# Value tiles on GpSimd's DMA queue, key tiles issued two pairs ahead on SyncE's: a decode attention kernel

## The chip, the cores and the metric

The kernel runs on one core of a Trainium2 chip. The metric is the device time of one execution in microseconds (us), and lower is better. Engines are called as in the profile: PE is TensorE (matmul), PEld its weight loads, DVE is VectorE, ACT is ScalarE, POOL is GpSimd, SP is SyncE. SP, ACT and POOL can issue DMAs, each on a queue of its own. The core has 16 DMA engines.

## The reference

One decode step of attention over a long cache, mixed with a small feed-forward block by a sigmoid gate. Everything is float32.

```python
# x [2,1,448], k_cache and v_cache [2,16,4096,256], wq [448,4096], wo [4096,448]
q = (x @ wq).reshape(B, Sq, H, Dh).transpose(0, 2, 1, 3)
scores = einsum("bhqd,bhkd->bhqk", q, k_cache) * (Dh ** -0.5)
p = softmax(scores)
a = einsum("bhqk,bhkd->bhqd", p, v_cache).transpose(0, 2, 1, 3).reshape(B, Sq, H * Dh) @ wo
b = relu(x @ w1 + b1) ** 2 @ w2 + b2          # w1 [448,1792], w2 [1792,448]
g = sigmoid((x * gate_w).sum(-1, keepdims=True))
out = g * a + (1 - g) * b
```

Each of the 2 x 16 = 32 pairs of batch and head has one query row, 4 MB of keys and 4 MB of values. These caches are 268 of the 290 MB that the kernel reads.

## The kernel before

The main loop runs over the 32 pairs, numbered i = 0 to 31 (batch inside, head outside; the last is `last` = 31). A tile `k0_14_0` holds the keys of batch 0, head 14, so of pair 28; `v1_13_0` the values of pair 27. One tile is 128 partitions x 8192 floats, the whole 4 MB of a pair, and comes with one DMA. Values of the last two pairs come in two and three pieces.

All large tiles (keys, values, and the weights wq, w1, w2, wo) share a ring of five slots of 4 MB (`slot`). A load waits until the tile that had its slot has been used up: keys until their reduction on DVE, values until their products on PE. All these loads are issued on SP's queue in program order, so that a load that waits for its slot also holds back those behind it.

What pair i goes through:

- `times_q(i, ...)` (L294): DVE multiplies the keys in place by the query, in three pieces of 1024, 3072 and 4096 columns; `row_sums(i)` (L300): DVE adds up each row of 256, which gives 4096 scores.
- `maximum(i)` (L304, L306) and `softmax(i)` (L312, L317): a maximum over all partitions with the help of PE, then exponentials on ACT. DVE's stream puts the first piece of `times_q(i + 1)` between the two, so the softmax of pair i also stands behind the arrival of the keys of pair i + 1.
- `values(i)` (L343): 32 PE matmuls of the probabilities with the value tile.

At the top of iteration i the kernel issues the keys of pair i + 1 and then the values of pair i (in iteration 29 the keys of 30 and 31 and then the values of 29). Weights follow at fixed iterations: w1 at 2, a first part of w2 at 4, a group of wo at 7, 15 and 23. The last group of wo stands between the two pieces of v30, the rest of w2 (L111) behind the values of 31. At the very end PE multiplies wo and w2 chunks into `fin` (L390), one chunk after the other as they arrive, and 4 KB of output go out.

POOL does six small set-up instructions at the start and nothing in the loop.

Of the kernel before, what the change touches and what calls it, by code (L numbers as in the profile page):

```python
# [16 lines left out]
def kernel(  # L17
# [14 lines left out]
    nc = tc.nc  # L32
# [10 lines left out]
    J = 32  # L43
    NCH = NK // J
    HG = 4
    NG = H // HG
# [22 lines left out]
    def slot(name):  # L69
        return ring.tile([P, J * DH], F32, name=name, tag="ring")  # L70
# [15 lines left out]
    def load_w1():  # L86
        t = slot("w1")
        nc.sync.dma_start(t[:, :2 * F], w1[:2 * P, :].rearrange("(p c) n -> p (c n)", c=2))
        nc.sync.dma_start(t[:, 2 * F:3 * F], w1[2 * P:R0, :])
        nc.sync.dma_start(t[:, 3 * F:3 * F + F // 2], w1[R0:, :].rearrange("r (s n) -> (r s) n", s=2))  # L90
        w1_t.extend([t[:, :F], t[:, F:2 * F], t[:, 2 * F:3 * F], t[:, 3 * F:3 * F + F // 2]])
# [4 lines left out]
    def w2_slot(lo, hi):  # L96
        t = slot(f"w2_{lo}")
        tv = t[:, :(hi - lo) * D].rearrange("p (c n) -> p c n", n=D)
        for c in range(lo, hi):
            w2_sb[c] = tv[:, c - lo, :]  # L100
        return tv

    def load_w2_early():
        tv = w2_slot(0, WH)
        nc.sync.dma_start(tv, w2_v[:, :WH, :])

    def load_w2_late():
        tv = w2_slot(WH, FC)
        at = [0, *W2_CUTS, FC - WH]
        for lo, hi in zip(at, at[1:]):  # L110
            nc.sync.dma_start(tv[:, lo:hi, :], w2_v[:, WH + lo:WH + hi, :])  # L111
# [9 lines left out]
    def load_wo(g):  # L121
        t = slot(f"wo{g}")
        tv = t[:, :HJ * D]
        if g < NG - 1:
            nc.sync.dma_start(tv, wo_g[g])
            wo_sb[g] = tv.rearrange("p (j n) -> p j n", j=HJ)
        else:
            nc.sync.dma_start(tv.rearrange("p (h k) -> p h k", h=HG), wo_v[:, g * HG:(g + 1) * HG, :])
            wo_sb[g] = tv.rearrange("p (h j n) -> p h j n", h=HG, j=NJ)

    def load_kv(src, i, nm, cuts=(), between=None):
        b, h = pairs[i]
        v = src[b, h].rearrange("(n p j) d -> n p j d", p=P, j=J)
        tiles = []
        for n in range(NCH):
            t = slot(f"{nm}{b}_{h}_{n}").rearrange("p (j d) -> p j d", d=DH)
            at = [0, *(cuts if n == NCH - 1 else ()), J]
            for lo, hi in zip(at, at[1:]):
                nc.sync.dma_start(t[:, lo:hi, :], v[n, :, lo:hi, :])
                if between is not None and hi < J:  # L140
                    between()
            tiles.append(t)
        return tiles

    pairs = [(b, h) for h in range(H) for b in range(B)]
    last = len(pairs) - 1
# [43 lines left out]
    for c in range(CF + 1):  # L190
        src = (x2[:, c:2 * P:2] if c < 2 else x2[:, c * P:(c + 1) * P] if c < CF
               else xr2.rearrange("b r s -> b (r s)"))
# [41 lines left out]
    def make_q(b, n):  # L234

        a, gq = divmod(n, 4)
        r = 32 * gq + b
        pq = ps.tile([P, 512], F32, name=f"pq{b}_{n}", tag="pq")
        nc.tensor.matmul(pq, ident[:, r:r + 1].to_broadcast([P, P]), qs[:, a, :], start=True, stop=True)  # L239
        t = work.tile([P, QB], F32, name=f"q{b}_{n}", tag=f"q{b}")  # L240
        nc.scalar.activation(t, pq, AF.Copy)  # L241
        for k in range(QH):
            q_sb[b, n * QH + k] = t[:, k * DH:(k + 1) * DH]
# [36 lines left out]
    kts, s_t, rs_t, rl_t, oT = {}, {}, {}, {}, {}  # L280
# [8 lines left out]
    def times_q(i, lo, hi):  # L289

        b, h = pairs[i]
        for n, a, e in parts(lo, hi):
            kt = kts[i][n][:, a:e, :]
            nc.vector.tensor_tensor(kt, kt, q_sb[b, h].unsqueeze(1).to_broadcast([P, e - a, DH]), op=ALU.mult)  # L294
# [7 lines left out]
    def maximum(i):  # L302
        m = work.tile([P, 1], F32, name=f"m{i}", tag="m")
        nc.vector.tensor_reduce(m, s_t[i], axis=AX.X, op=ALU.max)  # L304
        mt = ps.tile([P, 512], F32, name=f"mt{i}", tag="sm")
        nc.tensor.matmul(mt[:, :P], m.to_broadcast([P, P]), ident, start=True, stop=True)  # L306
        return mt

    def softmax(i, mt):
        b, h = pairs[i]  # L310
        nb = work.tile([P, 1], F32, name=f"nb{i}", tag="nb")
        nc.vector.tensor_reduce(nb, mt[:, :P], axis=AX.X, op=ALU.max, negate=True)  # L312
        u, k = unit_of[h]
        c = B * k + b
        if c == 0:
            rs_t[u] = work.tile([P, B * len(units[u])], F32, name=f"rs{u}", tag="rs")
        nc.scalar.activation(pw[k, b][:, :, 2 * c:2 * c + 2], s_t[i].rearrange("p (m s) -> p m s", s=2), AF.Exp,  # L317
                             bias=nb, accum_out=rs_t[u][:, c:c + 1])

    def sums(u):  # L320
        sm = ps.tile([P, 512], F32, name=f"sum{u}", tag="sm")
        nc.tensor.matmul(sm[:, :B * len(units[u])], ones_pp, rs_t[u], start=True, stop=True)  # L322
        return sm

    def norm(u, sm):
        n = len(units[u])
        rc = work.tile([P, n, B], F32, name=f"rc{u}", tag="rc")
        nc.vector.reciprocal(rc, sm[:, :B * n].rearrange("p (k b) -> p k b", b=B))
        nc.vector.tensor_tensor(rc, rc, gP[:, 0, :].unsqueeze(1).to_broadcast([P, n, B]), op=ALU.mult)
        rl = work.tile([P, n * B, 2], F32, name=f"rl{u}", tag="rl")  # L330
        nc.vector.tensor_tensor(rl, m16[:, :4 * n].rearrange("p (c s) -> p c s", s=2),
                                rc.rearrange("p k b -> p (k b)").unsqueeze(2).to_broadcast([P, n * B, 2]), op=ALU.mult)
        rl_t[u] = rl
# [49 lines left out]
    def project(g):  # L383
        for j in range(HJ):
            nc.tensor.matmul(acc[:, :D], oT[g][:, j, :], wo_sb[g][:, j, :], start=False,  # L385
                             stop=(g == NG - 2 and j == HJ - 1))
# [13 lines left out]


    kts[0] = load_kv(k_cache, 0, "k")
    project_q()
    make_q(0, 0)
# [9 lines left out]
            times_q(i, n * J, (n + 1) * J)  # L414
            row_sums(i, n * J, (n + 1) * J)

    for i, (b, h) in enumerate(pairs):

        for n in (range(i + 1, i + 2) if i < last - 2 else range(i + 1, last + 1) if i == last - 2 else ()):
            kts[n] = load_kv(k_cache, n, "k")  # L420
        if i == last - 1:
            vt = load_kv(v_cache, i, "v", (J // 2,), lambda: load_wo(NG - 1))
        else:
            vt = load_kv(v_cache, i, "v", (J // 2, 3 * J // 4) if i == last else ())
        if i == 2:
            load_w1()
        if i == 4:
            load_w2_early()
        grp = h // HG
        if b == B - 1 and h % HG == HG - 1 and grp < NG - 1:  # L430
            load_wo(grp)
        if i == last:
            load_w2_late()

        if i < last - 1:
            mt = maximum(i)
        if i < last:
            times_q(i + 1, 0, LEAD)
        softmax(i, mt)
        if i < last:  # L440
            times_q(i + 1, LEAD, LEAD2)
        u, k = unit_of[h]
        done = b == B - 1 and k == len(units[u]) - 1
        if done:
            norm(u, sums(u))


        if h % QH == QH - 1 and h + 1 < H:
            make_q(b, (h + 1) // QH)
        if k == 0 and b == 0 and u > 0:  # L450
            turn(u - 1)
            if u < NG:
                project(u - 1)
        if i == 3:
            ffn_hidden()
        if i == 4:
            pt = ffn_turn()
        if i == 5:
            for c in range(WH):
                nc.tensor.matmul(acc[:, :D], hT[:, c, :], w2_sb[c], start=False, stop=False)  # L460
        if i == last - 6:

            ya = const.tile([B, D], F32, name="ya")
            nc.scalar.activation(ya, acc[:, :D], AF.Copy)
        if i == last - 5:
            late(ident[:B, :B], ya, start=True)

        if i == last - 2:
            rest(i + 1)
            mt = maximum(i + 1)  # L470
        if i < last - 1:
            values(i, vt)
            if done:
                take(u)
        if i == last - 1:
            rest(last)
            values(i, vt, 0, NK // 4)
            values(i, vt, NK // 4, 3 * NK // 8 + 2)
            mt = maximum(last)
            values(i, vt, 3 * NK // 8 + 2)  # L480
        elif i < last - 2:
            rest(i + 1)
        if i == 4:
            ffn_square(pt)
# [46 lines left out]
```

## Time and profile before

| | |
|---|---|
| device time, median of 3 runs | 683.49 us (683.36 to 683.56) |
| profiled execution, its own time | 683.23 us |
| its span, first to last instruction | 681.4 us |
| read from HBM | 289.56 MB, 425 GB/s over the span |
| PE, DVE, ACT, POOL busy | 296.5, 581.1, 37.9, 0.7 us |

The span is what the trace shows of one execution; 1.8 us of the device time lie outside it. Rows of the timeline give the start, the duration, the engine, the line, the operation with its tiles, and in brackets the idle time of the engine just before it with what ended that idle time. An `x2` means that two instructions are merged into one row, from the start of the first to the end of the second. Rows of the DMA list give the size of one transfer and the median time from its issue to its landing. The chain of work that ended last is followed back from the last instruction. `SPq`, `ACTq` and `POOLq` are the instruction queues of the engines that issue DMAs.

### The profile page before, as it was taken

To read this page: it belongs to the slowest core of one execution; us is meant where nothing else is said; L and a number is where in the kernel's file an instruction comes from. 1 tells how busy PE (TensorE), PEld (TensorE's weight loads), DVE (VectorE), ACT (ScalarE), POOL (GpSimd) and SP (SyncE) were. 2 spreads that over 40 slices of the span, in tenths; PEclk is the share of its full clock that TensorE was granted. 3 is DMA by queue.
4 is the path that set the end of the run, shared out by engine and by line. 5 is a ranking of instruction groups with operands and counts; after the bars stand their busy time and mean duration, and the time that the engine had idled before them with its cause. 6 is when DMAs were issued, how large, how long until landed. Compare 5 with 4: busy or idle time off the path is not lost.

```text
span 681.4 us, 3865 instructions
## 1 busy us (share of the span) xinstructions
PE 296.5 (44%) x1598; PEld 96.8 (14%) x1598; DVE 581.1 (85%) x233; ACT 37.9 (6%) x113; POOL 0.7 (0%) x6
## 2 busy tenths in 40 slices
PE   4413445543359134433347543422455712443066
PEld 1000111400115001000014110000112200101013
DVE  3299997989896999999996999899997899999990
ACT  0200001000010000000001000000001000000000
POOL 0000000000000000000000000000000000000000
PEclk9856667787656776665667865567667757667579
DMA  8999999999999999999999999999999999999996
GB/s 370 435 433 435 430 425 431 426 434 436 431 437 430 431 431 431 430 431 431 432 426 441 431 431 432 433 429 431 431 430 423 432 431 431 430 435 437 423 419 270
DMA packets 12380, 289.79 MB, mean 425 GB/s; under 512 B 1478, under 2 KB 1612, under 8 KB 2892
## 3 DMA queue, kind: packets, MB, share of 16 engines
q1 hardware_dynamic: 12200, 289.55, 99.1%
q8 instruction: 12, 0.20, 0.1%
q10 hardware_dynamic: 164, 0.02, 0.0%
q14 instruction: 4, 0.03, 0.0%
HBM read 289.56 MB, written 0.00 MB: 425 GB/s over the span
## 4 chain that ended last, share of the span: by engine, by line
DMA 59%; DVE 37%; PE 2%; issue 0%; SPq 0%; ACT 0%; DVEq 0%; ACTq 0%
DMA k<-in_A_k_cache_dram 56%; DVE k L294 18%; DVE s L300 18%; DMA w<-in_B_w_dram 3%; PE acc L385 1%; PE po_buf L343 1%; DVE nb L312 0%; PE mt L306 0%; DVE m L304 0%; PE fin L390 0%; SPq L111 0%; ACT oT L378 0%; SPq L81 0%; ACT pw L317 0%; SPq L80 0%
## 5 line engine op out<-in xcount | busy, mean ns | idle before, releaser
L294 DVE TENSOR_TENSOR k<-k,q 128x3072 f32<-128x3072 f32 (+3 forms) x94 | 285.1, 3057 | 75.7 <-DMA k<-in_A_k_cache_dram 75.7
L300 DVE TENSOR_REDUCE s<-k 128x32 f32<-128x8192 f32 x32 | 278.0, 8686 | 2.2
L343 PE MATMUL po_buf<-v,pw 128*16 128x512 f32 (+2 forms) x1024 | 181.1, 857 | 218.3 <-DMA v<-in_A_v_cache_dram 217.4
L343 PEld LDWEIGHTS po_buf<-v,pw 128*16 128x16 f32 (+2 forms) x1024 | 36.7, 123 | 349.8 <-issue 319.7
L306 PE MATMUL mt<-ident,m 128*128 128x128 f32 x64 | 19.1, 389 | 136.2 <-DVE m L304 136.2
L317 ACT ACTIVATE pw<-s,nb 128x32 f32<-128x32 f32 x32 | 10.3, 323 | 544.0 <-DVE nb L312 544.0
L306 PEld LDWEIGHTS mt<-ident,m 128*128 128x128 f32 x64 | 11.9, 233 | 167.7 <-DVE m L304 117.1
L385 PE MATMUL acc<-wo,oT 128*2 128x448 f32 x48 | 22.9, 640 | 4.9 <-ACT oT L378 4.9
L239 PE MATMUL pq<-qs,ident 128*128 128x512 f32 x32 | 24.6, 868 | 0.0
L372 PEld LDWEIGHTS ot<-rl,shared 128*128 128x128 f32 x96 | 18.8, 304 | 0.0
L372 PE MATMUL ot<-rl,shared 128*128 128x8 f32 x96 | 18.8, 338 | 0.0
L312 DVE TENSOR_REDUCE nb<-mt 128x1 f32<-128x128 f32 x32 | 9.1, 284 | 1.7 <-PE mt L306 1.7
L241 ACT ACTIVATE q<-pq 128x512 f32<-128x512 f32 x16 | 9.4, 588 | 9.5 <-PE pq L239 9.5
L322 PE MATMUL sum<-rs,ones_pp 128*128 128x8 f32 (+2 forms) x10 | 2.8, 349 | 11.3 <-ACT pw L317 11.3
L354 ACT ACTIVATE shared<-po_buf 128x1024 f32<-128x1024 f32 x6 | 5.8, 1020 | 30.9 <-PE po_buf L343 30.9
L385 PEld LDWEIGHTS acc<-wo,oT 128*2 128x2 f32 x48 | 4.3, 94 | 21.3 <-issue 16.2
L239 PEld LDWEIGHTS pq<-qs,ident 128*128 128x128 f32 x32 | 6.9, 262 | 1.3 <-ACT qs L230 0.9
L269 PE MATMUL pt<-ident,shared 2*128 2x2 f32 x28 | 7.0, 378 | 0.0
L269 PEld LDWEIGHTS pt<-ident,shared 2*128 2x128 f32 x28 | 6.9, 336 | 0.1
L304 DVE TENSOR_REDUCE m<-s 128x1 f32<-128x32 f32 x32 | 5.9, 186 | 1.1
L317 ACT ACTIVATION_READ_ACCUMULATOR pw<-s,nb 128x1 f32 x32 | 6.0, 187 | 0.0
L228 PE MATMUL po_buf<-wqa,xT 128*2 128x512 f32 x32 | 5.6, 858 | 0.8 <-DMA wqa<-in_A_wq_dram 0.8
(62 smaller groups left out, 55.3 us busy)
## 6 DMA issues: line engine op xcount, KB each, us to landing
k<-in_A_k_cache_dram SPq DMA_DIRECT2D x32, 4096.0 KB, 40.0
v<-in_A_v_cache_dram SPq DMA_DIRECT2D x30, 4096.0 KB, 31.6
wo<-in_A_wo_dram SPq DMA_DIRECT2D x4, 1792.0 KB, 34.1
v<-in_A_v_cache_dram SPq DMA_DIRECT2D x3, 2048.0 KB, 25.9
wqa<-in_A_wq_dram SPq DMA_DIRECT2D x1, 4096.0 KB, 12.4
w<-in_B_w_dram SPq DMA_DIRECT2D x3, 896.0 KB
wqb<-in_A_wq_dram SPq DMA_DIRECT2D x1, 2048.0 KB, 16.9
v<-in_A_v_cache_dram SPq DMA_DIRECT2D x2, 1024.0 KB, 24.5
```

The lines of the kernel that those rows point to most:

```text
L239: nc.tensor.matmul(pq, ident[:, r:r + 1].to_broadcast([P, P]), qs[:, a, :], start=True, stop=True)
L241: nc.scalar.activation(t, pq, AF.Copy)
L269: nc.tensor.matmul(pt[:, c, :], hv[:, c, :], ident[:B, :B], start=True, stop=True)
L294: nc.vector.tensor_tensor(kt, kt, q_sb[b, h].unsqueeze(1).to_broadcast([P, e - a, DH]), op=ALU.mult)
L300: nc.vector.tensor_reduce(s_t[i][:, n * J + a:n * J + e], kts[i][n][:, a:e, :], axis=AX.X, op=ALU.add)
L304: nc.vector.tensor_reduce(m, s_t[i], axis=AX.X, op=ALU.max)
L306: nc.tensor.matmul(mt[:, :P], m.to_broadcast([P, P]), ident, start=True, stop=True)
L312: nc.vector.tensor_reduce(nb, mt[:, :P], axis=AX.X, op=ALU.max, negate=True)
L317: nc.scalar.activation(pw[k, b][:, :, 2 * c:2 * c + 2], s_t[i].rearrange("p (m s) -> p m s", s=2), AF.Exp, bias=nb, accum_out=rs_t[u][:, c ...
L343: nc.tensor.matmul(po[r:r + 4 * n, :], pw[k, b][:, m, :4 * n], vt[j // J][:, j % J:j % J + 2, :].rearrange("p j d -> p (j d)"), start=(k = ...
L372: nc.tensor.matmul(ptv[:, j, :], ov[:, s, j, :], rl_t[u][:, :, s], start=(s == 0), stop=(s == 1))
L385: nc.tensor.matmul(acc[:, :D], oT[g][:, j, :], wo_sb[g][:, j, :], start=False, stop=(g == NG - 2 and j == HJ - 1))
```

## The change

Values of pairs 1 to 28 are loaded through POOL's queue, as `load_kv` takes the queue as an argument. Their loads now stand in the code behind the softmax of the pair before, and the keys are issued for pair i + 2 at the top of iteration i. Values of pairs 0, 29, 30 and 31 and all weights stay on SP's queue. The number of tiles, slots and bytes is as before.

```diff
-    def load_kv(src, i, nm, cuts=(), between=None):
+    def load_kv(src, i, nm, cuts=(), between=None, queue=nc.sync):
...
-                nc.sync.dma_start(t[:, lo:hi, :], v[n, :, lo:hi, :])
+                queue.dma_start(t[:, lo:hi, :], v[n, :, lo:hi, :])
...
-        for n in (range(i + 1, i + 2) if i < last - 2 else range(i + 1, last + 1) if i == last - 2 else ()):
-            kts[n] = load_kv(k_cache, n, "k")
-        if i == last - 1:
-            vt = load_kv(v_cache, i, "v", (J // 2,), lambda: load_wo(NG - 1))
-        else:
-            vt = load_kv(v_cache, i, "v", (J // 2, 3 * J // 4) if i == last else ())
...
+    kts[1] = load_kv(k_cache, 1, "k")
+    vts = {0: load_kv(v_cache, 0, "v")}
+    for i, (b, h) in enumerate(pairs):
+
+        if i + 2 < last:
+            kts[i + 2] = load_kv(k_cache, i + 2, "k")
+        if i == last - 3:
+            kts[last] = load_kv(k_cache, last, "k")
 
         if i < last - 1:
             mt = maximum(i)
         if i < last:
             times_q(i + 1, 0, LEAD)
         softmax(i, mt)
+        if i < last - 2:
+            vts[i + 1] = load_kv(v_cache, i + 1, "v", queue=nc.gpsimd if i < last - 3 else nc.sync)
+            load_weights(i + 1)
+        if i == last - 2:
+            vts[i + 1] = load_kv(v_cache, i + 1, "v", (J // 2,), lambda: load_wo(NG - 1))
+            vts[last] = load_kv(v_cache, last, "v", (J // 2, 3 * J // 4))
+            load_w2_late()
+        vt = vts[i]
```

`load_weights(i)` is a new function that holds the loads of w1, the early part of w2 and the groups of wo that stood at the top of the loop. The order of SP's queue near the end, before, with the semaphores that each load waits for (DVE: the slot held keys that DVE has to finish; PE: it held values or weights that PE has to finish; DMAHW and DMASW: counters of earlier loads):

```order
L139 DMA v1_12_0_1221<-in_A_v_cache_dram 128x8192 [waits DMAHW5_49,PE_49]
L139 DMA k1_13_0_1253<-in_A_k_cache_dram 128x8192 [waits DMAHW6_49,PE_49]
L139 DMA v0_13_0_1255<-in_A_v_cache_dram 128x8192 [waits DMAHW0_49,PE_49]
L139 DMA k0_14_0_1293<-in_A_k_cache_dram 128x8192 [waits DMAHW7_49,DVE_49]
L139 DMA v1_13_0_1295<-in_A_v_cache_dram 128x8192 [waits DMAHW1_49,DVE_49]
L139 DMA k1_14_0_1329<-in_A_k_cache_dram 128x8192 [waits DMAHW2_49,PE_49]
L139 DMA v0_14_0_1331<-in_A_v_cache_dram 128x8192 [waits DMAHW3_49,DVE_49]
L139 DMA k0_15_0_1361<-in_A_k_cache_dram 128x8192 [waits DMAHW4_49,PE_49]
L139 DMA k1_15_0_1363<-in_A_k_cache_dram 128x8192 [waits DMAHW5_49,DVE_49]
L139 DMA v1_14_0_1365<-in_A_v_cache_dram 128x8192 [waits DMAHW6_49,PE_49]
```

Keys and values alternate in one queue, and both kinds take slots of either kind. SP's queue at the same place after the change:

```order
L139 DMA k0_13_0_1160<-in_A_k_cache_dram 128x8192 [waits DMASW4_49,DMASW2_49,DMASW6_49,DMASW0_49,PE_49]
L139 DMA k1_13_0_1223<-in_A_k_cache_dram 128x8192 [waits DMAHW7_49,PE_49]
L139 DMA k0_14_0_1257<-in_A_k_cache_dram 128x8192 [waits DMAHW0_49,DVE_49]
L139 DMA k1_14_0_1297<-in_A_k_cache_dram 128x8192 [waits DMAHW1_49,DVE_49]
L139 DMA k0_15_0_1333<-in_A_k_cache_dram 128x8192 [waits DMAHW5_49,DMAHW2_49,DVE_49]
L139 DMA k1_15_0_1335<-in_A_k_cache_dram 128x8192 [waits DMASW2_49,DMAHW6_49,DMASW0_49,PE_49]
L139 DMA v1_14_0_1345<-in_A_v_cache_dram 128x8192 [waits DMAHW3_49,DVE_49]
```

The keys of pairs 26 to 31 now follow each other without values between them, and the first values in this queue are those of pair 29. POOL's queue after the change, the last five loads (before, POOL issued none):

```order
L139 DMA v0_12_0_1125<-in_A_v_cache_dram 128x8192 [waits DMAHW5_49,DMAHW7_49,DMAHW2_49,DVE_49]
L139 DMA v1_12_0_1171<-in_A_v_cache_dram 128x8192 [waits DMAHW3_49,DMAHW6_49,DMAHW0_49,DVE_49]
L139 DMA v0_13_0_1233<-in_A_v_cache_dram 128x8192 [waits DMASW7_49,PE_49]
L139 DMA v1_13_0_1267<-in_A_v_cache_dram 128x8192 [waits DMASW0_49,PE_49]
L139 DMA v0_14_0_1307<-in_A_v_cache_dram 128x8192 [waits DMASW1_49,PE_49]
```

The values of pairs 24 to 28 stand alone here. From pair 26 on a value tile takes the slot of the value tile two pairs before it (it waits for PE), so that these values rotate through two slots and keys through the others.

More of the change, by code (lines that the diff above doesn't have):

```diff
@@ L415, in rest, with load_weights @@
             row_sums(i, n * J, (n + 1) * J)
-    for i, (b, h) in enumerate(pairs):
-        for n in (range(i + 1, i + 2) if i < last - 2 else range(i + 1, last + 1) if i == last - 2 else ()):
-            kts[n] = load_kv(k_cache, n, "k")
-        if i == last - 1:
-            vt = load_kv(v_cache, i, "v", (J // 2,), lambda: load_wo(NG - 1))
-        else:
-            vt = load_kv(v_cache, i, "v", (J // 2, 3 * J // 4) if i == last else ())
+    def load_weights(i):
+        b, h = pairs[i]
         if i == 2:
@@ L431 @@
             load_wo(grp)
-        if i == last:
-            load_w2_late()
+    kts[1] = load_kv(k_cache, 1, "k")
[5 more added lines that the diff above has]
+            kts[last] = load_kv(k_cache, last, "k")
         if i < last - 1:
```

## The prediction

> **What bounds the kernel now.** I read the page first: the engines, the DMA row, the queues and the chain that ended last.
>
> ```profile
> span 681.4 us, 3865 instructions
> PE 296.5 (44%) x1598; PEld 96.8 (14%) x1598; DVE 581.1 (85%) x233; ACT 37.9 (6%) x113; POOL 0.7 (0%) x6
> DMA  8999999999999999999999999999999999999996
> GB/s 370 435 433 435 430 425 431 426 434 436 431 437 430 431 431 431 430 431 431 432 426 441 431 431 432 433 429 431 431 430 423 432 431 431 430 435 437 423 419 270
> ...
> q1 hardware_dynamic: 12200, 289.55, 99.1%
> q10 hardware_dynamic: 164, 0.02, 0.0%
> ...
> DMA 59%; DVE 37%; PE 2%; issue 0%; SPq 0%; ACT 0%; DVEq 0%; ACTq 0%
> L294 DVE TENSOR_TENSOR k<-k,q 128x3072 f32<-128x3072 f32 (+3 forms) x94 | 285.1, 3057 | 75.7 <-DMA k<-in_A_k_cache_dram 75.7
> ```
>
> SP's queue (q1) keeps the 16 DMA engines 99.1% busy, and no slice between the first and the last has a gap. VectorE is the next resource: 581.1 us busy, of its idle time 75.7 us are waits for keys. The average over the stage without ends, by windows:
>
> ```profile
> 10.00:650.00 640.00, 273.12 (x1329) 86.27 (x1332) 560.66 (x203) 33.92 (x102) 0.00 (x0) 0.65 1.00 431
> ```
>
> 431 GB/s at a DMA share of 1.00: there is no idle transfer time to win, so the change can gain only by a higher rate, and otherwise matters by the order in which tiles land. That order I read near the end, where nothing later can make up for it: SP's issues, then VectorE's first multiply of each pair and TensorE's value products, with the idle time before each.
>
> ```profile
> 567.64 0.33 SPq L139 DMA_DIRECT2D v<-in_A_v_cache_dram  x1
> 568.06 0.38 SPq L139 DMA_DIRECT2D k<-in_A_k_cache_dram  x1
> 587.08 0.33 SPq L139 DMA_DIRECT2D v<-in_A_v_cache_dram  x1
> 587.50 19.34 SPq L139 DMA_DIRECT2D k<-in_A_k_cache_dram  x2
> 606.93 19.36 SPq L139 DMA_DIRECT2D v<-in_A_v_cache_dram  x2
> 626.38 0.39 SPq L128 DMA_DIRECT2D wo<-in_A_wo_dram  x1
> 626.82 20.39 SPq L139 DMA_DIRECT2D v<-in_A_v_cache_dram  x4
> 653.13 3.70 SPq L111 DMA_DIRECT2D w<-in_B_w_dram  x4
> ```
> ```profile
> 569.23 1.23 DVE L294 TENSOR_TENSOR k<-k,q 128x1024 f32<-128x1024 f32 x1 [1.40 <-DMA k<-in_A_k_cache_dram]
> 588.73 1.23 DVE L294 TENSOR_TENSOR k<-k,q 128x1024 f32<-128x1024 f32 x1 [1.46 <-DMA k<-in_A_k_cache_dram]
> 608.18 1.23 DVE L294 TENSOR_TENSOR k<-k,q 128x1024 f32<-128x1024 f32 x1 [1.48 <-DMA k<-in_A_k_cache_dram]
> 627.58 1.22 DVE L294 TENSOR_TENSOR k<-k,q 128x1024 f32<-128x1024 f32 x1 [1.43 <-DMA k<-in_A_k_cache_dram]
> 646.04 1.22 DVE L294 TENSOR_TENSOR k<-k,q 128x1024 f32<-128x1024 f32 x1
> 663.88 0.19 DVE L304 TENSOR_REDUCE m<-s 128x1 f32<-128x32 f32 x1
> ```
> ```profile
> 579.05 5.92 PE L343 MATMUL po_buf<-v,pw 128*12 128x512 f32 x32 [9.46 <-DMA v<-in_A_v_cache_dram]
> 598.48 6.44 PE L343 MATMUL po_buf<-v,pw 128*12 128x512 f32 x32 [8.66 <-DMA v<-in_A_v_cache_dram]
> 617.92 5.27 PE L343 MATMUL po_buf<-v,pw 128*12 128x512 f32 x32 [10.68 <-DMA v<-in_A_v_cache_dram]
> ```
>
> With k(i), v(i) for the tiles of pair i: the issues are v27, k29, v28, k30, k31, v29, half of v30, wo, the rest of v30 with v31, w2. They land strictly in that order, one per 9.7 us: k27 569.2, v26 579.0, k28 588.7, v27 598.5, k29 608.2, v28 617.9, k30 627.5. VectorE gets every key tile just after it has asked for it (1.4 us idle), then runs pairs 30 and 31 without a wait: 663.88 - 627.58 = 36.30, so 18.15 us a pair. The keys of k31 overtake v29 already in the code, which is why there is no wait at 646.04.
>
> Behind 663.88 the end is bound nearly twice over, as TensorE's rows there and the chain's last transfer show:
>
> ```profile
> 668.83 0.11 PEld L343 LDWEIGHTS po_buf<-v,pw 128*4 128x4 f32 x8 [0.92 <-DMA v<-in_A_v_cache_dram]
> 671.32 1.04 PE L343 MATMUL po_buf<-v,pw 128*4 128x512 f32 x8 [0.68 <-DMA v<-in_A_v_cache_dram]
> 675.68 0.95 PE L390 MATMUL fin<-w,hT 128*2 128x112 f32 x32 [0.24 <-DMA w<-in_B_w_dram]
> 677.32 0.95 PE L390 MATMUL fin<-w,hT 128*2 128x112 f32 x32 [0.68 <-DMA w<-in_B_w_dram]
> ```
> ```profile
> 653.98 23.29 DMA w<-in_B_w_dram
> ```
>
> The last transfer lands at 677.27 (653.98 + 23.29) and 4.1 us follow. But from the last key reduction on TensorE waits for DMA only 0.92 + 0.68 + 0.24 + 0.68 = 2.5 us in all. So the last scores may be 2.5 us later at no cost, and every further microsecond is one of the span.
>
> **The change, part by part.** *Bytes:* the same 289.55 MB on the same 16 engines. Cost 0 at an unchanged rate. The DMAs on q1 fall by 28; no row shows what rate a load from POOL's queue has. Bounds from the rows: nothing, to 2% either way on 28 x 9.7 = 272 us, 5.4 us (the inner slices of the GB/s row lie between 419 and 441, some 2% around 431). I take 0, because the rate is set by 16 busy engines and not by who issues.
>
> *Issue time:* SP loses 28 issues of 0.33 to 0.38 us, 10 us in all, hidden now by about two loads in the queue. POOL gains them; it is idle after its six instructions (0.7 us). An issue there is priced by no row: between 0 and one whole VectorE instruction, should it be held up by one. In the second half two value tiles have slots, so the next load is queued while one moves; nothing waits for the issue. 0.
>
> *SP's queue order:* before, k(i+2) stood behind v(i+1) and its wait for a slot. Now SP holds keys and weights alone, POOL values alone, and each issues when its own slot is free. Weights (w1, early w2, wo) stay among the keys, and slow keys only. What is queued behind a waiting SP issue is the next key tile; behind a waiting POOL issue, the next values.
>
> *Landing order:* this is the term. Two queues that both hold work share the engines. The trace has one place where they did:
>
> ```profile
> wqa<-in_A_wq_dram SPq DMA_DIRECT2D x1, 4096.0 KB, 12.4
> b1T<-in_B_b_dram ACTq DMA_DIRECT2D x1, 7.0 KB, 14.9
> ```
>
> b1T is 128 rows of 56 bytes, 8 for each DMA engine, and took 14.9 us beside wqa and wqb. A 4 MB tile is 8 rows of 32 KB for each engine in 9.7 us, 1.2 us a row; 14.9 us is some 12 such rows. So tiny rows waited about one large row each: the engines take the two queues in turn, row by row. The Trainium skill, "DMA: Bandwidth & Descriptors", section "Queues, rings and completion order", says that an engine drains a whole packet, typically 9 to 17 descriptors, before it switches; by that b1T's 8 rows would have gone in one turn, which the 14.9 us speak against. (By that rule for POOL's packets the sum would be that of the second rival.)
>
> Rows of k and v have one size, so turn by turn each queue gets half. Then a value tile that used to follow its key tile moves beside it, and both land when the later did: v27 with k28 at 598.5, v28 with k29 at 617.9. The bytes landed by then are the same as before. v28 is not too late for that: its slot is free when the products of v26 are done, and these need only k27 (569.2), the 1.2 us multiply, its softmax and 5.9 us of products: near 578. After 617.9 SP is alone: k30 at 627.5 as now.
>
> VectorE: k28 from 598.5 to 616.6, then k29 from 617.9, k30 and k31 without a wait: 617.9 + 3 x 18.15 = 672.4 for the last reduction, against 663.88: +8.5. Put otherwise, one value tile ahead of the keys (+9.7) less the waits of 1.4 that it swallows. Less the 2.5 us of cover at the end: **+6.0 us**. The late transfers stay on time: v31 takes the slot of k30, free at 654.2, while the queue ahead of it is busy until 661.4; w2's slot is v29's, whose products wait for v29 itself, as now.
>
> Sum: 0 + 0 + 6.0. The profiled execution took 683.23 us with its span of 681.4 (1.8 us around it), so 689.2; the median 683.49 is 0.26 above that execution, too little to matter. Bounds of the term: 0 if the keys stay first, 14.4 if two value tiles get ahead (below).
>
> **Rivals.** *Keys stay ahead, no change.* If POOL's loads start late or get less than half of the turns, values fall behind, as now, and k28 and k29 land by 588.7 and 608.2 or earlier. The end is then the last transfer, 677.27 + 4.1, whatever VectorE gains: 683.2, the side that is not slower. It decides at just under half: the lead of keys over values grows or shrinks by the difference in turns, and 28 tiles add up. For it: POOL's loads may start a microsecond or two later than SP's. Against: a queued second value tile hides that. A rule of the Trainium skill bears on it: "SBUF — State Buffer", section "Who interferes with whom", lets VectorE block GpSimd's descriptor writing in some modes, but counts tensor_reduce as never contending and tensor_tensor as leaving it unharmed; by that nothing is delayed here. Should a reduction hold it anyway, values come up to 8.7 us later and the keys gain; no row here shows either.
>
> *Values get more turns.* If POOL's turn is several rows, v27 and v28 land ahead of k28: 588.7 + 2 x 9.7 = 608.2 for k28, then 4 x 18.15 = 680.8 for the last reduction, +16.9 - 2.5 = +14.4: 697.6. For it: values are held back only by their slots. Against: b1T's row by row turns.
>
> *The rate changes.* 2% less on POOL's loads: +5.4, about 688.6 with keys ahead. Faster needs both a rate above 431 and keys ahead: 1% over 570 us with two queues gives -5.7, 677.5. For it: two queues could close gaps between rows. Against: share 1.00 already.
>
> **How the numbers follow.** Turn by turn sharing, +6.0: 0.42, its own range 686.5 to 691.5. Values further ahead: 0.12. Rate loss: 0.08. Together slower by over 0.2% (1.4 us, what a measurement can tell from no change): 0.62. Keys ahead at the same rate: 0.26, same. Faster by the rate: 0.12. The range leaves out the faster case and part of the second rival: 682.3 to 697.6.
>
> **What would show it.** Right: in the last fifth VectorE's waits for keys are as many, but k29 lands near 618 with v28 beside it; landing times of both kinds near 30 us and no order between them; the last reduction near 672; TensorE's waits for values nearly gone (now 8.7 to 10.7 a pair); TensorE waiting for scores and not for w2 at the end; DMA share still 1.00. Wrong: the last reduction at or before 664 with the chain's end on w2 (keys ahead), DMA digits under 9 in the middle (starved queues), or a mean above 435 GB/s.

## The result and the profile after

The changed kernel takes 690.19 us (median of 4 runs, 688.23 to 692.63) against 683.44 us before (4 runs, 683.36 to 683.56): ratio 1.010, 95% interval 1.0068 to 1.0133. It is slower, by 6.8 us. The runs also lie some twenty times as far apart as those of the kernel before (4.4 us for 0.2).

The page of the changed kernel, the lines that answer to those of before. Its execution took 690.25 us, 1.8 us more than its span, as before.

```profile
span 688.5 us, 3894 instructions
PE 301.0 (44%) x1598; PEld 103.2 (15%) x1598; DVE 580.0 (84%) x233; ACT 38.1 (6%) x113; POOL 15.6 (2%) x34
DMA  9999999999999999999999999999999999999993
...
q1 hardware_dynamic: 8168, 172.10, 58.5%
q0 software_dynamic: 4032, 117.44, 39.7%
...
DMA 51%; DVE 39%; PE 8%; issue 1%; ACT 0%; SPq 0%; DVEq 0%; POOLq 0%; ACTq 0%
L294 DVE TENSOR_TENSOR k<-k,q 128x3072 f32<-128x3072 f32 (+3 forms) x94 | 285.1, 3057 | 84.5 <-DMA k<-in_A_k_cache_dram 84.5
L343 PE MATMUL po_buf<-v,pw 128*16 128x512 f32 (+2 forms) x1024 | 172.6, 816 | 74.9 <-DMA v<-in_A_v_cache_dram 59.5
L139 POOL DMA_DIRECT2D v<-in_A_v_cache_dram x28 | 14.9, 533 | 573.0 <-PE po_buf L343 327.0
```

The engines that move data are busy up to the last slice but one, as before. POOL's queue (q0) moved 117.44 MB in 39.7% of 16 engines' 688.5 us, 26.9 GB/s per engine; SP's queue 172.10 MB in 58.5%, 26.7 GB/s; before, 289.55 MB in 99.1%, 26.8 GB/s. So the software queue moves a byte as fast as the hardware queue, and issuing costs POOL, which has little else to do, 0.53 us a load. What changed is who waits. VectorE waits 8.8 us longer for keys, in 12 waits instead of 28 (before, then after; us in total, times, the longest):

```profile
DVE k L294 <- DMA k<-in_A_k_cache_dram: 75.7, 28, 20.1
```
```profile
DVE k L294 <- DMA k<-in_A_k_cache_dram: 84.5, 12, 23.9
```

TensorE waits far less for values: 59.5 us instead of 217.4, which the waits of the kernel before showed as

```profile
PE po_buf L343 <- DMA v<-in_A_v_cache_dram: 217.4, 27, 10.7
```

The changed kernel's VectorE towards the end, the first multiply of the pairs that waited, and the last reduction:

```profile
513.77 1.23 DVE L294 TENSOR_TENSOR k<-k,q 128x1024 f32<-128x1024 f32 x1 [1.45 <-DMA k<-in_A_k_cache_dram]
545.47 1.23 DVE L294 TENSOR_TENSOR k<-k,q 128x1024 f32<-128x1024 f32 x1 [13.20 <-DMA k<-in_A_k_cache_dram]
...
671.42 0.19 DVE L304 TENSOR_REDUCE m<-s 128x1 f32<-128x32 f32 x1
```

and the same place before, pairs 25 and 26:

```profile
530.59 1.23 DVE L294 TENSOR_TENSOR k<-k,q 128x1024 f32<-128x1024 f32 x1 [6.31 <-DMA k<-in_A_k_cache_dram]
549.79 1.23 DVE L294 TENSOR_TENSOR k<-k,q 128x1024 f32<-128x1024 f32 x1 [1.24 <-DMA k<-in_A_k_cache_dram]
```

The keys of pair 25 come 14.9 us later (545.47 for 530.59), one and a half tiles. From there VectorE runs through seven pairs without one wait for keys. Before, it waited 1.24 + 1.40 + 1.46 + 1.48 + 1.43 = 7.0 us on the way. 14.9 - 7.0 is 7.9, and the last reduction is 7.5 us later (671.42 for 663.88). The chain that ended last shows why pair 25's keys were late:

```profile
501.11 6.38 PE po_buf L343 x32
507.48 0.02 issue
507.50 37.84 DMA k<-in_A_k_cache_dram
```

They could be issued only when TensorE had used up a value tile (507.48), and then took 37.84 us for 4 MB that alone take 9.7: in front of them on SP's queue stood the third group of wo, beside them on POOL's two value tiles. That group is 1.8 MB in rows of 14 KB. It landed 35.0 us after its issue at 492.69, at 527.7. The keys ahead of it, those of pair 24, were in by 513.77, when VectorE took them up. What the two queues moved from 513.2 to 527.2 (packets, MB, share of the engines):

```profile
q0 software_dynamic: 133, 3.83, 63.8%
q1 hardware_dynamic: 142, 2.16, 36.1%
```

Each queue got about as many packets as the other, but most of SP's are small here. So SP's queue moved 2.16 MB, where half of 431 GB/s would have given it 3.0 MB, and the group landed some 14 us behind the keys ahead of it; alone it takes 4.3 us.

### The profile page after: what moved, and what is told of

Same layout as the page of the kernel before. It is cut to its first block, busy times and chain, and to the rows that moved or that the text cites. A ratio compares the mean times of both kernels' runs of the same rounds, so it can differ in the third digit from the quotient of the medians.

```text
span 688.5 us, 3894 instructions
## 1 busy us (share of the span) xinstructions
PE 301.0 (44%) x1598; PEld 103.2 (15%) x1598; DVE 580.0 (84%) x233; ACT 38.1 (6%) x113; POOL 15.6 (2%) x34
## 3 DMA queue, kind: packets, MB, share of 16 engines
q1 hardware_dynamic: 8168, 172.10, 58.5%
q0 software_dynamic: 4032, 117.44, 39.7%
## 4 chain that ended last, share of the span: by engine, by line
DMA 51%; DVE 39%; PE 8%; issue 1%; ACT 0%; SPq 0%; DVEq 0%; POOLq 0%; ACTq 0%
DMA k<-in_A_k_cache_dram 27%; DMA v<-in_A_v_cache_dram 25%; DVE k L294 19%; DVE s L300 19%; PE po_buf L343 6%; PE fin L390 1%; PE pq L239 0%; DVE nb L312 0%; PE mt L306 0%; DVE m L304 0%; PE ot L372 0%; ACT o L358 0%; ACT q L241 0%; PE sum L322 0%; SPq L81 0%
## 5 line engine op out<-in xcount | busy, mean ns | idle before, releaser
L294 DVE TENSOR_TENSOR k<-k,q 128x3072 f32<-128x3072 f32 (+3 forms) x94 | 285.1, 3057 | 84.5 <-DMA k<-in_A_k_cache_dram 84.5
L343 PE MATMUL po_buf<-v,pw 128*16 128x512 f32 (+2 forms) x1024 | 172.6, 816 | 74.9 <-DMA v<-in_A_v_cache_dram 59.5
L306 PE MATMUL mt<-ident,m 128*128 128x128 f32 x64 | 25.2, 497 | 270.6 <-DVE m L304 270.6
L306 PEld LDWEIGHTS mt<-ident,m 128*128 128x128 f32 x64 | 15.9, 309 | 300.6 <-DVE m L304 220.8
L239 PE MATMUL pq<-qs,ident 128*128 128x512 f32 x32 | 29.2, 1019 | 0.0
L139 POOL DMA_DIRECT2D v<-in_A_v_cache_dram x28 | 14.9, 533 | 573.0 <-PE po_buf L343 327.0
L372 PEld LDWEIGHTS ot<-rl,shared 128*128 128x128 f32 x96 | 20.8, 333 | 0.0
L372 PE MATMUL ot<-rl,shared 128*128 128x8 f32 x96 | 20.5, 357 | 0.0
L241 ACT ACTIVATE q<-pq 128x512 f32<-128x512 f32 x16 | 9.5, 591 | 14.6 <-PE pq L239 14.6
L239 PEld LDWEIGHTS pq<-qs,ident 128*128 128x128 f32 x32 | 8.3, 315 | 1.3 <-ACT qs L230 0.9
## 6 DMA issues: line engine op xcount, KB each, us to landing
w<-in_B_w_dram SPq DMA_DIRECT2D x3, 896.0 KB, 17.1
```

The source lines that it names most:

```text
L139: queue.dma_start(t[:, lo:hi, :], v[n, :, lo:hi, :])
L343: nc.tensor.matmul(po[r:r + 4 * n, :], pw[k, b][:, m, :4 * n], vt[j // J][:, j % J:j % J + 2, :].rearrange("p j d -> p (j d)"), start=(k = ...
L372: nc.tensor.matmul(ptv[:, j, :], ov[:, s, j, :], rl_t[u][:, :, s], start=(s == 0), stop=(s == 1))
```

## Experiments

Eight kernels, in two groups of four, each group compared with the kernel before on the same chip.

**All on SP's queue, in the new order of the code.**

```diff
-            vts[i + 1] = load_kv(v_cache, i + 1, "v", queue=nc.gpsimd if i < last - 3 else nc.sync)
+            vts[i + 1] = load_kv(v_cache, i + 1, "v")
```

> The changed kernel with the values of pairs 1 to 28 back on SP's queue; keys two pairs ahead and the new place of the value loads stay. Theory of turns (two queues share the engines row by row, so a value tile moves beside or ahead of the keys that VectorE needs): one queue is first in, first out again, the landing order is that of before, 683 to 684 us, last key reduction near 664. Rival of the order (the new place of the issues is what costs): near 690. Rival of the software queue (POOL's loads are slower in themselves): 683 to 684 too.

Measured: 683.43 us, ratio 1.000 (0.9991 to 1.001). VectorE's waits for keys:

```profile
DVE k L294 <- DMA k<-in_A_k_cache_dram: 75.8, 28, 20.0
```

28 waits and 75.8 us, the pattern of before. The new places of the issues and the keys two pairs ahead do nothing by themselves; the rival of the order is out.

**All on POOL's queue, in the order of before.** The kernel before with `nc.gpsimd` for `nc.sync` in every large load.

> The kernel before with all large loads, keys, values and weights, on POOL's queue, in the order of before: one queue, but the software one. Theory of turns: with one queue there is nothing to share, 683 to 685 us (the first load may start a microsecond later). Rival of the software queue: all 290 MB pay, so if POOL's 117 MB cost the 7 us of the change, this costs 7 x 290 / 117 = 17 us, near 700.

Measured: 684.96 us, ratio 1.0022 (1.0012 to 1.0031). Its queue, its first issue and its last transfer in the chain:

```profile
q0 software_dynamic: 11728, 289.54, 98.8%
```
```profile
1.25 0.66 POOL L78 DMA_DIRECT2D wqa<-in_A_wq_dram  x1 [0.80 <-POOLq L517]
```
```profile
655.52 22.97 DMA w<-in_B_w_dram
```

The whole 290 MB went through the software queue. The first issue came at 1.25 instead of 0.74, after POOL's set-up, and the last transfer landed at 678.49 (655.52 + 22.97) instead of 677.27: 1.2 us later, which with little else is the 1.5 us. The rival asked for 17 us; the software queue is not what costs.

**Values on ACT's queue, a hardware queue.** The change with `nc.scalar` for `nc.gpsimd`.

> The changed kernel with the values of pairs 1 to 28 on ACT's queue, a hardware queue like SP's. Theory of turns: as with POOL's queue, 688 to 693 us, with single long waits of VectorE for keys behind the weights. Rival of the software queue: 683 to 684.

Measured: 692.93 us, ratio 1.0136 (1.0121 to 1.0151). Two hardware queues lose as much and a little more. That ACT, which also makes the exponentials, now issues loads is not what costs: TensorE waited 12.9 us for exponentials, against 14.6 us in the change. VectorE at the end, pairs 28 and 29 and the last reduction:

```profile
600.45 1.23 DVE L294 TENSOR_TENSOR k<-k,q 128x1024 f32<-128x1024 f32 x1 [1.75 <-DMA k<-in_A_k_cache_dram]
619.84 1.23 DVE L294 TENSOR_TENSOR k<-k,q 128x1024 f32<-128x1024 f32 x1 [1.43 <-DMA k<-in_A_k_cache_dram]
...
674.02 0.19 DVE L304 TENSOR_REDUCE m<-s 128x1 f32<-128x32 f32 x1
```

The keys of pair 29 come at 619.8 (before 608.2, forecast for POOL's queue 617.9), with a small wait in each of the pairs 27 to 29. This is the picture that the prediction drew. The "single long waits behind the weights" that were expected here are not the end of its story: 8.9 us stand at pair 25, but the last small wait, at pair 29, decides.

**Value tiles in halves, rows of 16 KB.**

```diff
-            vts[i + 1] = load_kv(v_cache, i + 1, "v", queue=...)
+            vts[i + 1] = load_kv(v_cache, i + 1, "v", (J // 2,) if i < last - 3 else (), queue=...)
```

> The changed kernel, but each value tile on POOL's queue comes as two DMAs of 16 KB rows, where keys keep rows of 32 KB. Theory of turns: a turn of POOL now moves half as much as one of SP, values get about a third, keys lead again, the last key reduction is at or before 664 and the time 683 to 685 us. If the engines shared by bytes instead of by rows, or if the software queue is what costs: 690 or more, as before this edit.

Measured: 696.50 us, ratio 1.019 (1.0174 to 1.0205). A miss: the time went up and not down. What VectorE waited for:

```profile
DVE nb L312 <- PE mt L306: 47.4, 13, 10.4
DVE k L294 <- DMA k<-in_A_k_cache_dram: 41.3, 4, 22.0
```

The waits for keys did halve, from 84.5 to 41.3 us, so the keys did get ahead. In their place stand 47.4 us of waits for the maximum over the partitions, which the change hardly had (0.9 us). The rows of TensorE and VectorE at one such wait:

```profile
599.26 3.61 PE L343 MATMUL po_buf<-v,pw 128*12 128x512 f32 x16 [10.91 <-DMA v<-in_A_v_cache_dram]
602.79 0.80 PE L306 MATMUL mt<-ident,m 128*128 128x128 f32 x2
```
```profile
603.63 0.29 DVE L312 TENSOR_REDUCE nb<-mt 128x1 f32<-128x128 f32 x1 [10.08 <-PE mt L306]
```

Here TensorE stood 10.91 us before the second half of a value tile, and the small matmul of the next maximum stands behind those products in its stream. VectorE needs that maximum to go on and stood with it. Late values stop VectorE as well as late keys do. The last reduction moved to 676.87. What the two queues moved from 560 to 612 us, while both held work:

```profile
q1 hardware_dynamic: 510, 15.14, 67.6%
q0 software_dynamic: 511, 7.34, 33.2%
```

The packets, most of them rows of tiles, are equal in number, and the bytes are two to one. So values got the third that was expected; what failed is the step from there to the time.

**Key tiles in halves, rows of 16 KB.** The mirror: `kts[i + 2] = load_kv(k_cache, i + 2, "k", (J // 2,) ...)` for pairs 2 to 28.

> The changed kernel with the key tiles of pairs 2 to 28 as two DMAs of 16 KB rows on SP's queue; values keep rows of 32 KB on POOL's. Theory of turns by rows: keys now get a third of the engines while both queues hold work, so they fall further behind: VectorE's waits for keys grow above the 84.5 us of the change and the time is 692 to 698. A rival by which the engines share by bytes: 688 to 692, unchanged.

Measured: 696.95 us, ratio 1.0197 (1.0182 to 1.0213).

```profile
DVE k L294 <- DMA k<-in_A_k_cache_dram: 87.8, 18, 23.8
```
```profile
592.58 4.42 DVE L294 TENSOR_TENSOR k<-k,q 128x4096 f32<-128x4096 f32 x1 [9.93 <-DMA k<-in_A_k_cache_dram]
...
678.35 0.19 DVE L304 TENSOR_REDUCE m<-s 128x1 f32<-128x32 f32 x1
```

As expected: the halves with small rows fall behind, now the keys, whose second half kept VectorE waiting 9.93 us as late as pair 27. The same bytes at the same rate, cut in two on the one queue or on the other, moved the time by 6 to 7 us beyond the change. The queues from 562 to 604 us:

```profile
q0 software_dynamic: 399, 12.03, 66.6%
q1 hardware_dynamic: 403, 5.82, 32.5%
```

Again the packets are equal in number, and now SP has half of the bytes of POOL. With the window of the value halves this shows that two busy queues share by rows and not by bytes.

**Weights behind the values on POOL's queue.** The change with `nc.gpsimd` for the loads of w1, the first part of w2 and the three groups of wo.

> The changed kernel with w1, the early part of w2 and the three groups of wo on POOL's queue, behind the values. VectorE's last long wait in the change (13.2 us for the keys of pair 25, landed at 545.3) stands behind wo2 on SP's queue: 1.8 MB, 4.3 us alone and twice that at half rate. Theory: what holds up the keys is the weights among them at half rate, so the keys of pair 25 land some 8 us earlier, the last reduction moves from 671.4 to 664 or less, 683 to 685 us. Rival (sharing alone, one value tile beside each key tile, sets the last reduction, as the prediction had it): still 688 to 692.

Measured: 689.03 us, ratio 1.0083 (1.0068 to 1.0098). The first half of the theory held, the second did not:

```profile
528.15 1.23 DVE L294 TENSOR_TENSOR k<-k,q 128x1024 f32<-128x1024 f32 x1 [0.40 <-DMA wo<-in_A_wo_dram]
...
556.46 0.29 DVE L312 TENSOR_REDUCE nb<-mt 128x1 f32<-128x128 f32 x1 [5.01 <-PE mt L306]
...
670.45 0.19 DVE L304 TENSOR_REDUCE m<-s 128x1 f32<-128x32 f32 x1
```

The keys of pair 25 are there at 528.1, 17 us earlier than in the change, so their delay did come from the weights among the keys. But now the weights hold up the values, and VectorE pays through TensorE: behind the arrival of pair 25 it waited 11.8 us for maxima, and 4.1 us before the first multiply of pair 26. Its waits in the whole kernel:

```profile
DVE k L294 <- DMA k<-in_A_k_cache_dram: 55.0, 17, 23.9
DVE nb L312 <- PE mt L306: 23.0, 10, 6.1
```

The last reduction is at 670.45, a microsecond earlier than in the change. The weights decide which tile is late, not whether one is.

**Shared queues only in the first part, and only in the last.** The change with POOL's queue for pairs 1 to 20, and then for pairs 21 to 28 alone.

```diff
-... queue=nc.gpsimd if i < last - 3 else nc.sync)
+... queue=nc.gpsimd if i < 20 else nc.sync)              # first kernel
+... queue=nc.gpsimd if 20 <= i < last - 3 else nc.sync)  # second kernel
```

> The changed kernel with POOL's queue for the values of pairs 1 to 20 only, SP's from 21 on. Theory: VectorE has 1.4 us to spare a pair when keys land in order, so what it loses before pair 20 is made good and only the order behind it counts: 683 to 684.5 us. Rival (something lost all along the way, such as rate or issue time): two thirds of the 7 us remain, near 688.

> The reverse: SP's queue for the values up to pair 20, POOL's for pairs 21 to 28. Theory: the whole loss comes back, 687 to 691 us, with one long wait for the keys of pair 25. Rival (loss all along the way): a third of it, near 685.5.

Measured: 684.13 us for the first, ratio 1.0018 (1.0008 to 1.0028), and 687.99 us for the second, ratio 1.0069 (1.0052 to 1.0086). Of the 6.8 us, some 0.7 remain when the values from pair 21 on are back on SP's queue, and 4.5 are there when only those of pairs 21 to 28 are on POOL's. The order near the end thus makes up most of the loss, though the two parts do not add up to the whole. The runs of the first spread from 683.82 to 686.33, so now and then something is left over. The end of the second kernel:

```profile
615.51 1.23 DVE L294 TENSOR_TENSOR k<-k,q 128x1024 f32<-128x1024 f32 x1 [1.47 <-DMA k<-in_A_k_cache_dram]
...
669.71 0.19 DVE L304 TENSOR_REDUCE m<-s 128x1 f32<-128x32 f32 x1
```

Here the last wait is for the keys of pair 29, at 615.5, where the prediction had it. The long wait expected at pair 25 did not come; one of 18.15 us stood at pair 22, where the sharing begins.

## Why the prediction was right

**What bounds it, and the sum.** The forecast was 689.2 us, +6.0; measured were 690.19 for the median and 690.25 for the profiled execution, whose span grew by 7.1.

- *Bytes, rate, issue time, taken at 0:* right. 26.7 to 26.9 GB/s for each engine on every queue, and 1.5 us for the whole program on POOL's queue. That a next value load is always queued while one moves did not hold: the one issued at 532.34 landed after 24.1 us, at 556.4, and POOL issued the next at 559.46. In these 3 us SP's keys had the engines alone.
- *Turn by turn sharing that puts a value tile beside the keys:* right as a mechanism. One queue, of either kind, gives 683.4 and 685.0; two, of either kind, 690.2 and 692.9. It is shown by the kernels that undo it, and the two windows with half rows show that the shares go by rows. That a turn is one row is shown by the kernel before, at the start, where b1T's rows of 56 bytes went beside rows of 32 KB. From 6 to 12 us SP's queue moved 80 packets and ACT's (q10) 78, one small row for each large one:

```profile
q1 hardware_dynamic: 80, 2.62, 101.1%
q10 hardware_dynamic: 78, 0.01, 1.1%
```

- *The size of the landing term:* forecast +8.5 us for the last reduction (672.4), measured +7.5 (671.42).
- *Its place:* wrong for this kernel. The prediction put the last wait at pair 29, with k29 and v28 landing together at 617.9. The trace has k29 at 614.6 (issued at 581.3) and v28 at 622.9 (issued at 588.75):

```profile
DMA to landing us min/median/max: 33.3/33.3/33.3
```
```profile
DMA to landing us min/median/max: 34.2/34.2/34.2
```

  VectorE came to k29 only at 617.1 and did not wait. The deciding wait was four pairs earlier, behind a group of wo: the prediction said that weights slow only the keys and then did not price it, and by turns of one row the 14 KB rows of wo slow them more than half a share would. Its sign of as many waits for keys in the last fifth failed too: before there were five, from 549.8 to 627.6, after there was none behind 545.5. A tile and a half there, less five small waits, came to about what one tile less one wait gave at pair 29. The number was therefore partly luck; on ACT's queue and with POOL's queue from pair 21 the deciding wait is where it was forecast.
- *The cover of 2.5 us at the end:* mis-sized, 0.4 measured (17.5 us from the last reduction to the end before, 17.1 after). TensorE's waits for the last weights did go, but the same 24 products took 1.1 us longer, half of what is missing:

```profile
666.95 2.93 PE L343 MATMUL po_buf<-v,pw 128*4 128x512 f32 x24
```
```profile
674.71 4.01 PE L343 MATMUL po_buf<-v,pw 128*4 128x512 f32 x24
```

  These are the products of the last pair before and after. The windows of the six microseconds behind the last reduction (before, then after; the third number from the end is the granted clock) show a lower clock:

```profile
663.88:670.00 6.12, 6.12 (x52) 1.74 (x51) 0.97 (x5) 0.41 (x2) 0.00 (x0) 0.86 1.00 416
```
```profile
671.42:677.50 6.08, 5.84 (x24) 1.63 (x28) 0.97 (x5) 0.41 (x2) 0.00 (x0) 0.52 0.82 334
```

  Before, TensorE had been at work since 661.4, 2.4 us ahead of the last reduction; after, it had stood 7.1 us and got a clock of 0.52 instead of 0.86. All ten traces fall in line: over the 6.1 us behind the last reduction the clock is 0.72 to 0.91 in the four whose TensorE was at work as it came, and 0.50 to 0.67 in the six where it had stood for 5.4 to 7.1 us. The two errors, +1.0 in the landing term and +2.1 in the cover, have opposite effects on the sum: 7.5 - 0.4 = 7.1.

**The rivals.** Keys ahead at no cost (0.26) fell in a way that was not foreseen: the kernel that puts keys ahead by smaller value rows is the second slowest of all, since values that are late stop VectorE through the order of TensorE's stream. So that rival had its price wrong: both sides of the balance cost. Values with more turns came out near their price when the keys' rows were halved: 696.95 for a forecast of 697.6. The last reduction is at 678.35 there, not at 680.8, and the last wait at pair 27, not at pair 28, so the close number is partly luck. The rate did not change in either direction. VectorE's 84% load of multiplies and reductions did not hold up POOL's issues: they take 0.53 us each and 0.67 us at most, in line with what the Trainium skill says of these operations in "SBUF — State Buffer", section "Who interferes with whom".

**What stays open.** Whether the idle stretch alone lowers TensorE's clock was not tried. Why single runs of the two-queue kernels differ by up to 4.4 us was not tried either. It may be that the order in which tiles land now depends on small differences in time; no run shows it.

No kernel here beats the one before. Its transfers fill 99.1% of the engines' time, and its one queue lets tiles land in the order in which they are used.

## What to carry to other kernels

Where the transfer engines are already full, a second queue moves no more bytes; it only changes the order in which they land, and turn by turn sharing of rows of one size makes both tiles finish when the later one would have. If the consumers use tiles in a fixed order with little to spare (1.4 us of 19.4 a pair here), issue them in that order on one queue. To see it in a profile, look for the engine whose many short waits for data became a few long ones, and add up its waits from the last long one to the end.

## What the runs showed of the hardware that was not expected

- A load of 290 MB through POOL's software queue ran at the rate of SP's hardware queue (98.8% and 99.1% of the engines' time for the same bytes). An issue took 0.53 us there and 0.33 us on SP.
- The share of a queue follows the size of its rows: with the rows of one of two busy queues halved, the two moved equal numbers of packets (510 and 511, 399 and 403) and bytes in the ratio of two to one. Beside values in rows of 32 KB, SP's queue with weights in rows of 14 KB got 36.1% of the engines.
- TensorE's granted clock in the last 6 us was 0.52 where it had stood 7.1 us before, and 0.86 where it was already at work; 24 matmuls took 4.01 us for 2.93.
